# Another plan of products, and the second mixing three steps after the first

## The chip, the cores and the metric

The kernel runs on one core of one Trainium2 chip. The metric is the device time of one execution in microseconds. TensorE (PE in the profile) multiplies, VectorE (DVE), ScalarE (ACT) and GpSimd (POOL) work on elements, SyncE (SP) issues most of the transfers. A matmul writes to PSUM, a memory of eight banks; "PEld" in the rows is the loading of a stationary operand.

## What is computed

Talking-heads attention over 4 batches, 12 heads, 448 positions and a head size of 64, and behind it a feed-forward block with a squared ReLU:

```python
scores = scale * np.matmul(q, k.transpose(0, 1, 3, 2))
scores = np.einsum('bhij,hg->bgij', scores, w_pre)      # first mixing, over heads
scores = scores - np.max(scores, axis=-1, keepdims=True)
attn = np.exp(scores)
attn = attn / (np.sum(attn, axis=-1, keepdims=True) + 1e-09)
attn = np.einsum('bhij,hg->bgij', attn, w_post)         # second mixing, over heads
x = np.matmul(attn, v)          # then to (4 * 448, 768)
h = x @ w_in                    # (768, 2048)
r = np.maximum(h, 0.0)
out = (s * (r * r) + b) @ w_out
```

All inputs and the output are float32. To keep that accuracy the kernel splits operands into a high and a low part and forms each product as three matmuls (low x high, high x low, high x high).

## The kernel before

The 448 query rows of a batch are cut into 4 chunks of 110 or 118 rows, 16 chunks in all, and a chunk into 11 or 12 **blocks** of up to 10 rows. There are 180 blocks; 10 rows times 12 heads give the 120 partitions on which both mixings work. `first[c]` is the first block of chunk c; the last chunk, 15, begins at block 168.

The work on a block t, in order:

- `relayout` (a transfer) and `split` (two GpSimd operations) bring its scores to 120 partitions, as `hl`.
- `premix(t)`, the first mixing: three matmuls into a PSUM slot `pm`; VectorE takes the maximum (L570, "reduction" in the text), ScalarE the exponential (L575) with its sum, and a small scaling of that sum, `st` (L579).
- `normalize(t)`: VectorE's reciprocal (L587), then ScalarE writes the high half of `eh` (L589). `remainder(t)`: VectorE writes the low half of `eh` (L596), the last reader of the `pm` slot. There are three `pm` slots, two from block 168 on.
- `postmix(t)`, the second mixing: twelve small matmuls from `eh` into a slot `po` (L611). `evacuate(t)` copies `po` into the chunk's tile `A`, on VectorE (L627), for the last chunk on ScalarE (L625).

The products that feed and follow the blocks belong to pairs of heads: `qk_pair` (QK in the text) makes scores of a coming chunk in the two PSUM banks `sc`, from which ScalarE copies them to `S` (L495); `av_pair` (AV) multiplies a finished chunk with the values, into `xp`; `prep_q` and `prep_k` transpose Q and K on TensorE, also through `sc`: ScalarE copies the high part out (L444, L464) and VectorE subtracts for the low part (L233), which stays in the list `later` until the next call of `low_parts`. Q of a chunk is transposed in two halves, of four and of two pairs of heads. `head_piece` is a part of the first feed-forward product. `convert_step` issues one operation of the conversion of weights, on VectorE: one per step from step 12 on for seven units of weights, and three per step from step 169 on for three further units.

One loop runs over steps s. Its body, for a step in the middle, issues in this order, and each engine runs what it is given in that order:

```python
        relayout(s + LD); split(s + LS)        # 5 and 2 blocks ahead
        convert_step(NU_EARLY); normalize(s - 1)
        low_parts()
        evacuate(s - 3)
        premix(s)
        remainder(s - 1)
        run_plan(s, True)                      # transfers
        postmix(s - 2)
        run_plan(s, False)                     # transpositions, QK, AV, head pieces
```

What `run_plan` issues in a step stands in a list `plan`, which is made ahead by a small planner: each product has a step at which it is due, the earliest and the last step, and a cost; a step takes products, in order of their due times, while `spent` is below `FILL`. A step may be left without any product ("empty" in the text).

## Time and profile before

| | |
|---|---|
| time, three runs | median 989.76 us (988.83 to 989.76) |
| the profiled execution | 989.5 us, its span 987.8 us |
| TensorE busy | 935.6 us, mean granted clock 0.987 of full |
| VectorE, ScalarE, GpSimd busy | 641.9, 607.9, 399.3 us |
| first reduction of a block | at 32.03 us |
| first AV of the last chunk | at 510.89 us |

The time of an execution is a little longer than its span, which goes from the first to the last instruction. The block steps lie between about 30 and 511 us of the span; behind them follow the feed-forward products. Busy time of TensorE counts matmuls, which overlap, with modelled ends, so what a step costs there is better read from the starts of its matmuls.

### The profile page before, as it was taken

The numbers are of one execution on the slowest core, as the hardware profiler recorded it, in microseconds if no ns is written. First come the engines' busy times: TensorE is split into PE (matmuls) and PEld (weight loads), VectorE is DVE, ScalarE is ACT, GpSimd is POOL, SyncE is SP. The second block draws the span as 40 slices with busy tenths as digits, with TensorE's granted clock in tenths as the row PEclk, the third lists the DMA queues.
The fourth block names the chain that finished last, engine by engine and source line by source line (L and its number), as shares of the span: only waits on it lengthen the run. The fifth ranks groups of instructions, "written<-read, shape, count | busy, mean of one in ns | idle before, by whom it ended". The sixth has DMA issues, their size and how long they took to land.

```text
span 987.8 us, 19819 instructions
## 1 busy us (share of the span) xinstructions
PE 935.6 (95%) x7500; PEld 792.3 (80%) x7500; DVE 641.9 (65%) x1314; ACT 607.9 (62%) x1315; POOL 399.3 (40%) x469
## 2 busy tenths in 40 slices
PE   6798999989999999999799999999999999999998
PEld 3566777757777677777578999899998999999998
DVE  4689999977877787888945605937624911748411
ACT  3587878877888788887658778622215687721000
POOL 2666667756676666767423333200001232310000
PEclk9899999999999999999799999999999999999999
DMA  3565544664346543544511412325441330236521
GB/s 87 150 177 140 142 126 132 173 153 128 103 123 159 131 134 102 141 128 136 168 56 38 142 34 77 92 91 158 134 155 33 106 119 1 64 113 187 164 94 53
DMA packets 124222, 114.63 MB, mean 116 GB/s; under 512 B 61626, under 2 KB 120014, under 8 KB 124126
## 3 DMA queue, kind: packets, MB, share of 16 engines
q1 hardware_dynamic: 115902, 102.26, 37.3%
q10 hardware_dynamic: 8064, 11.01, 3.1%
q8 instruction: 59, 0.97, 0.4%
q0 software_dynamic: 160, 0.09, 0.2%
q14 instruction: 37, 0.30, 0.1%
HBM read 58.28 MB, written 16.52 MB: 76 GB/s over the span
## 4 chain that ended last, share of the span: by engine, by line
PE 52%; ACT 21%; DVE 18%; DMA 5%; issue 2%; SPq 1%; POOL 1%; ACTq 0%; DVEq 0%; POOLq 0%
PE po L300 23%; PE ph L248 16%; ACT pm L575 6%; ACT S L495 5%; DVE st L570 4%; PE xp L509 4%; PE pm L568 3%; DVE A L627 3%; ACT eh L589 3%; ACT st L579 2%; DMA blk<-S 2%; PE sc L485 2%; PE po L611 2%; DVE eh L596 2%; DVE raw L172 1%
## 5 line engine op out<-in xcount | busy, mean ns | idle before, releaser
L300 PE MATMUL po<-w,g 128*128 128x384 f32 x1344 | 234.6, 336 | 2.6 <-ACT h L256 2.6
L300 PEld LDWEIGHTS po<-w,g 128*128 128x128 f32 x1344 | 233.6, 188 | 3.3 <-ACT h L256 3.2
L556 POOL TENSOR_TENSOR hl<-blk,hl 120x448 fp32r<-120x448 f32 x180 | 207.5, 1153 | 15.0
L266 POOL TENSOR_TENSOR g<-h,g 128x448 fp32r<-128x448 f32 x64 | 77.2, 1206 | 293.9 <-ACT g L265 275.4
L555 POOL TENSOR_SCALAR hl<-blk 120x448 fp32r<-120x448 f32 x180 | 105.0, 583 | 158.3 <-PE pm L568 137.4
L248 PE MATMUL ph<-x,w 128*128 128x448 f32 x810 | 166.2, 364 | 0.0
L611 PEld LDWEIGHTS <-eh 120*128 120x128 f16 (+1 forms) x2160 | 118.0, 99 | 56.0 <-DVE eh L596 27.0
L248 PEld LDWEIGHTS ph<-x,w 128*128 128x128 f32 x810 | 152.0, 188 | 12.2
L611 PE MATMUL po<-wpost,eh 120*128 120x120 f16 (+1 forms) x2160 | 148.2, 220 | 10.5 <-DVE eh L596 10.2
L575 ACT ACTIVATE pm<-pm,st 120x448 f32<-120x448 f32 x180 | 109.7, 609 | 76.3 <-DVE st L570 75.4
L596 DVE SCALAR_TENSOR_TENSOR eh<-pm,st,eh 120x448 f16<-120x448 f32 x180 | 122.1, 678 | 15.0 <-ACT eh L589 10.9
L589 ACT ACTIVATE eh<-pm,st 120x448 f16<-120x448 f32 x180 | 114.5, 636 | 15.2 <-DVE st L587 14.2
L570 DVE TENSOR_REDUCE st<-pm 120x1 f32<-120x448 f32 x180 | 110.8, 616 | 11.5 <-PE pm L568 10.9
L627 DVE COPY A<-po 128x480 f32<-128x480 f32 x168 | 107.3, 639 | 0.1
L568 PE MATMUL pm<-hl,wpre_hi 120*120 120x448 f32 x360 | 104.4, 372 | 1.8 <-POOL hl L556 1.8
L485 PE MATMUL sc<-Tk,Tq 64*110 64x448 f32 (+1 forms) x576 | 84.9, 401 | 13.1 <-ACT S L495 6.1
L509 PE MATMUL xp<-A,v 128*64 128x110 f32 (+1 forms) x1536 | 92.3, 266 | 1.0 <-ACT xs L523 1.0
L154 ACT ACTIVATE mk<-raw 128x384 f32<-128x384 f32 x64 | 35.4, 553 | 92.8 <-DMA raw<-in_moe_w_out_dram 38.1
L568 PE MATMUL pm<-hl,wpre_lo 120*120 120x448 f32 x180 | 84.3, 468 | 5.9 <-DVE eh L596 5.3
L495 ACT ACTIVATE S<-sc 110x896 f32<-110x896 f32 (+1 forms) x90 | 82.1, 912 | 8.8 <-PE sc L485 5.4
L509 PEld LDWEIGHTS xp<-A,v 128*64 128x64 f32 x1536 | 74.8, 137 | 15.7 <-issue 8.5
L568 PEld LDWEIGHTS pm<-hl,wpre_hi 120*120 120x120 f32 x360 | 67.0, 187 | 7.2 <-POOL hl L556 2.8
(72 smaller groups left out, 971.3 us busy)
## 6 DMA issues: line engine op xcount, KB each, us to landing
blk<-S SPq DMA_DIRECT2D x172, 210.0 KB
raw<-in_moe_w_in_dram SPq DMA_DIRECT2D x32, 384.0 KB
raw<-in_moe_w_out_dram SPq DMA_DIRECT2D x32, 384.0 KB
xraw<-xd SPq DMA_DIRECT2D x48, 224.0 KB
part<-ob ACTq DMA_DIRECT2D x28, 192.0 KB
acc<-part SPq DMA_DIRECT2D x28, 192.0 KB
out_dram<-acc ACTq DMA_DIRECT2D x28, 192.0 KB
v<-in_v_dram SPq DMA_DIRECT2D x24, 192.0 KB
```

The source lines that it names most:

```text
L248: nc.tensor.matmul(ph[:, :S], w[:, i, c0:c0 + P], x[:, y, :], start=(kc == 0 and m == 0), stop=(kc == NKC - 1 and m == 2),)
L300: nc.tensor.matmul(po[:, :NO], g[:, x, c0:c0 + P], w[:, y, :], start=(f == 0 and m == 0), stop=(f == NF - 1 and m == 2),)
L495: nc.scalar.activation(s_t[ci][:n, 2 * p:2 * p + 2, :], x_t["two"][:n, :, :S], AF.Copy, scale=SCALE)
L509: nc.tensor.matmul(xp[e * D:(e + 1) * D, p % 4, :n], vt[:, e, c, :], a[:, c, 2 * p + e, :n], start=(c == 0), stop=(c == NC - 1),)
L556: nc.gpsimd.tensor_tensor(out=hl[:n, 1, :], in0=blk[:n], in1=hl[:n, 0, :].bitcast(F32), op=ALU.subtract)
L568: nc.tensor.matmul(pm[:n, :S], w[:n, :n], hl[:n, x, :], start=(m == 0), stop=(m == 2))
L570: nc.vector.tensor_reduce(out=st[:n, 0:1], in_=pm[:n, :S], axis=AX.X, op=ALU.max, negate=True)
L575: nc.scalar.activation(e[:n], e[:n], AF.Exp, bias=st[:n, 0:1], accum_out=pm[:n, S:S + 1])
L589: nc.scalar.activation(eh[:n, 0, :], e[:n], AF.Copy, scale=st[:n, 3:4])
L596: nc.vector.scalar_tensor_tensor(out=eh[:n, 1, :], in0=e[:n], scalar=st[:n, 3:4], in1=eh[:n, 0, :], op0=ALU.mult, op1=ALU.subtract,)
L611: nc.tensor.matmul(po[:, c * BP:(c + 1) * BP], eh[:n, x, j0:j0 + P], wpost[:n, y].rearrange("p g i -> p (g i)"), start=(m == 0), stop=(m = ...
L627: nc.vector.tensor_copy(dst, src)
```

## The change

The second mixing of a block, `postmix`, is issued three steps after the first mixing instead of two, and `evacuate` four instead of three; the loop has one step more, and the bounds of the AV pairs and head pieces are one step later. `eh` has three buffers instead of two, and the transposed K tiles `Tk` seven instead of eight. The planner has other costs, and a product is taken if half its cost still fits under `FILL`, where before it was taken while anything was left. No operation is added or removed.

```diff
--- before.py
+++ after.py
@@ -440,7 +440,7 @@
                 nat[:n, c].rearrange("p h d -> p (h d)"),
                 ident[:n, :n],
             )
-        t = qkp.tile([P, 2, S], F32R, tag="Tk", name=f"Tk_{b}_{p}", bufs=8)
+        t = qkp.tile([P, 2, S], F32R, tag="Tk", name=f"Tk_{b}_{p}", bufs=7)
         nc.scalar.activation(t[:, 0, :], tr[:, :S], AF.Copy)
         later.append((t[:, 1, :], tr[:, :S], t[:, 0, :]))
         k_t[b, p] = t
@@ -585,7 +585,7 @@
         n = blocks[t][2] * H
         e, st = e_t[t]
         nc.vector.reciprocal(st[:n, 3:4], st[:n, 2:3])
-        eh = blkp.tile([BP, 2, S], F16, tag="eh", name=f"eh_{t}", bufs=2)
+        eh = blkp.tile([BP, 2, S], F16, tag="eh", name=f"eh_{t}", bufs=3)
         nc.scalar.activation(eh[:n, 0, :], e[:n], AF.Copy, scale=st[:n, 3:4])
         eh_t[t] = eh
 
@@ -628,8 +628,9 @@
 
     LD, LS = 5, 2
     CONV0 = 12
-    FILL = 1.33
-    QK_COST, AV_COST = 0.8, 1.3
+
+    FILL = 1.2
+    QK_COST, AV_COST, PREP_COST = 0.9, 0.95, 0.5
     LATE = 6
 
 
@@ -649,7 +650,7 @@
         step = math.floor(step)
         while load.keys() & {step - 1, step, step + 1}:
             step -= 1
-        load[step] = 0.375
+        load[step] = PREP_COST
         at(step, 1, f, *args)
         return step
 
@@ -672,10 +673,10 @@
             fill.append((when, lo, w1 - 1, QK_COST, 1, qk_pair, (ci, p)))
     for ci in range(NCH):
         b = chunks[ci][0]
-        w0 = first[ci + 1] + 3
-        w1 = first[ci + 2] + 3 if ci + 2 <= NCH else NB + 100
+        w0 = first[ci + 1] + 4
+        w1 = first[ci + 2] + 4 if ci + 2 <= NCH else NB + 100
         if ci == NCH - 1:
-            w0 = NB + 3
+            w0 = NB + 4
         for p in range(NP):
             when = w0 + p * min(w1 - w0, 12) / NP
             fill.append((when, w0, w1 - 1, AV_COST, 1, av_pair, (ci, p)))
@@ -684,13 +685,14 @@
     w0 = first[NCH - 1] + 3
     for i in range(NHEAD * NKC):
         if i < NHEAD * NKC - LATE:
-            when = w0 + i * (NB + 3 - w0) / (NHEAD * NKC - LATE)
-            fill.append((when, w0, NB + 2, 0.567, 1, head_piece, ()))
+            when = w0 + i * (NB + 4 - w0) / (NHEAD * NKC - LATE)
+            lo = first[NCH - 1] + max(4, 2 + min(i, NKC - 1))
+            fill.append((when, lo, NB + 3, 0.567, 1, head_piece, ()))
         else:
-            fill.append((NB + 100, NB + 3, NB + 100, 0.567, 1, head_piece, ()))
+            fill.append((NB + 100, NB + 4, NB + 100, 0.567, 1, head_piece, ()))
     fill.sort(key=lambda x: x[0])
     spent, closed = 0.0, {}
-    for s in range(NB + 4):
+    for s in range(NB + 5):
         spent = max(spent, -0.4) + load.get(s, 0)
         left, held = [], set()
         for x in fill:
@@ -698,12 +700,12 @@
             waits = f in held
 
             opens = f is qk_pair or (f is av_pair and args[1] % 4 == 0)
-            if opens and closed.get(f, -1) >= s and s <= NB + 2 and s < hi:
+            if opens and closed.get(f, -1) >= s and s <= NB + 3 and s < hi:
                 waits = True
 
             if f is qk_pair and s in load and s < hi:
                 waits = True
-            if not waits and lo <= s and (s > NB + 2 or hi <= s or (x[0] < s + 4 and spent < FILL)):
+            if not waits and lo <= s and (s > NB + 3 or hi <= s or (x[0] < s + 4 and spent + cost / 2 <= FILL)):
                 at(s, order, f, *args)
                 spent += cost
                 if f is qk_pair or (f is av_pair and args[1] in (3, NP - 1)):
@@ -772,7 +774,7 @@
         x[3](*x[4])
         low_parts()
     tail = first[NCH - 1]
-    for s in range(NB + 3):
+    for s in range(NB + 4):
         if s == tail - LD:
             early.close()
             rp = ctx.enter_context(tc.tile_pool(name="rp", bufs=1, side="right", reuse_waits="tile"))
@@ -791,15 +793,15 @@
                     convert_step(NU_EARLY + 3)
             normalize(s - 1)
         low_parts()
-        if 0 <= s - 3 < NB:
-            evacuate(s - 3)
+        if 0 <= s - 4 < NB:
+            evacuate(s - 4)
         if s < NB:
             premix(s)
         if 0 <= s - 1 < NB:
             remainder(s - 1)
         run_plan(s, True)
-        if 0 <= s - 2 < NB:
-            postmix(s - 2)
+        if 0 <= s - 3 < NB:
+            postmix(s - 3)
         run_plan(s, False)
         if 0 <= s - (tail - LD) < NKC:
             load_x(0, 0, s - (tail - LD))
```

TensorE's order at a change of batch, steps 62 and 63 (the steps begin at the rows `pm`, the first mixing; `po` is the second mixing, of which one row stands here; `trk` a transposition of K, `sc` a QK pair, `xp` an AV pair). Before:

```order
L568 MATMUL pm_3112<-hl_3010,wpre_lo 120x448
L568 MATMUL pm_3112<-hl_3010,wpre_hi 120x448 x2
...
L438 MATMUL trk_3_3138<-ident,nk_3_2852 128x128 x3
L438 MATMUL trk_3_3138<-ident,nk_3_2852 128x64
L568 MATMUL pm_3155<-hl_3063,wpre_lo 120x448
L568 MATMUL pm_3155<-hl_3063,wpre_hi 120x448 x2
...
L485 MATMUL sc_0_3178<-Tk_0_1355,Tq_3046 118x448 x6
L509 MATMUL xp_4_3186<-A_2435,v_4_2917 64x110 x8
```

The same two steps of the change:

```order
L568 MATMUL pm_3080<-hl_2974,wpre_lo 120x448
L568 MATMUL pm_3080<-hl_2974,wpre_hi 120x448 x2
...
L438 MATMUL trk_3_3106<-ident,nk_3_2815 128x128 x3
L438 MATMUL trk_3_3106<-ident,nk_3_2815 128x64
L509 MATMUL xp_0_3017<-A_2445,v_2_2751 64x110 x8
L568 MATMUL pm_3131<-hl_3033,wpre_lo 120x448
L568 MATMUL pm_3131<-hl_3033,wpre_hi 120x448 x2
...
L485 MATMUL sc_0_3154<-Tk_0_1331,Tq_3010 118x448 x6
```

The AV pair now stands behind the transposition, ahead of the next first mixing, and the QK pair of step 63 is alone.

TensorE's order where a chunk's AV pairs begin, steps 103 to 105. Before:

```order
L568 MATMUL pm_4912<-hl_4819,wpre_lo 120x448
...
L568 MATMUL pm_4944<-hl_4862,wpre_lo 120x448
...
L509 MATMUL xp_0_4966<-A_4433,v_0_4542 64x110 x8
L509 MATMUL xp_0_4966<-A_4433,v_1_4629 64x110 x8
L568 MATMUL pm_4997<-hl_4905,wpre_lo 120x448
...
L460 MATMUL trq_0_5024<-ident,nq_4739 128x118 x4
L509 MATMUL xp_0_4966<-A_4433,v_2_4716 64x110 x8
```

The same steps of the change:

```order
L568 MATMUL pm_4886<-hl_4782,wpre_lo 120x448
...
L485 MATMUL sc_5_4908<-Tk_5_3952,Tq_4495 110x448 x6
L568 MATMUL pm_4929<-hl_4840,wpre_lo 120x448
...
L568 MATMUL pm_4961<-hl_4879,wpre_lo 120x448
...
L460 MATMUL trq_0_4988<-ident,nq_4712 128x118 x4
L509 MATMUL xp_0_4994<-A_4442,v_0_4552 64x110 x8
```

Before, step 103 is empty and step 104 holds two AV pairs; in the change a QK pair stands in step 103, step 104 is empty and step 105 holds one AV pair.

VectorE's order in step 170, in the last chunk (from its reduction on; L176, L178 and L155 are conversion, `x_0_2` the low part of an input of the feed-forward block). Before:

```order
L570 TENSOR_REDUCE st_7785<-pm_7781 120x1
L596 SCALAR_TENSOR_TENSOR eh_7777<-pm_7742,st_7746,eh_7777 120x448
L176 TENSOR_SCALAR u_7733<-w_7731 128x384
L178 SCALAR_TENSOR_TENSOR w_7731<-raw_2685,u_7733 128x384
L155 TENSOR_SCALAR u_7819<-raw_3014 128x384
L587 RECIPROCAL st_7785<-st_7785 120x1
L233 TENSOR_TENSOR x_0_2_7804<-xraw_0_2_7611,x_0_2_7804 128x448
L570 TENSOR_REDUCE st_7831<-pm_7827 120x1
```

The same of the change:

```order
L570 TENSOR_REDUCE st_7771<-pm_7767 120x1
L596 SCALAR_TENSOR_TENSOR eh_7763<-pm_7728,st_7732,eh_7763 120x448
L176 TENSOR_SCALAR u_7719<-w_7717 128x384
L178 SCALAR_TENSOR_TENSOR w_7717<-raw_2660,u_7719 128x384
L155 TENSOR_SCALAR u_7804<-raw_2978 128x384
L587 RECIPROCAL st_7771<-st_7771 120x1
L233 TENSOR_TENSOR x_0_2_7789<-xraw_0_2_7597,x_0_2_7789 128x448
L627 COPY A_7374<-po_7776 128x48x10
L570 TENSOR_REDUCE st_7816<-pm_7812 120x1
```

One evacuation more runs on VectorE here, since the evacuation of the last chunk, which is ScalarE's, begins a step later.

## Rows read from the trace of the kernel before

**Rows 1.** The page's first part: busy us of each engine, share of the span, instructions.

```profile
PE 935.6 (95%) x7500; PEld 792.3 (80%) x7500; DVE 641.9 (65%) x1314; ACT 607.9 (62%) x1315; POOL 399.3 (40%) x469
```

**Rows 2.** Busy time by stretches: length; PE, PEld, DVE, ACT, POOL; clock; transfers' share, GB/s.

```profile
63.91:157.58 93.67, 87.92 (x965) 64.34 (x964) 86.93 (x186) 75.70 (x182) 61.73 (x70) 1.00 0.50 135
...
250.37:315.15 64.78, 63.58 (x730) 47.80 (x728) 51.98 (x110) 52.55 (x128) 44.46 (x58) 1.00 0.48 125
```

**Rows 3.** Groups between 63.91 and 466.95: busy, mean ns | idle before, releaser.

```profile
L611 PE MATMUL po<-wpost,eh 120*128 120x120 f16 x1788 | 119.8, 217 | 6.9 <-DVE eh L596 6.7
...
L570 DVE TENSOR_REDUCE st<-pm 120x1 f32<-120x448 f32 x148 | 91.1, 616 | 6.3 <-PE pm L568 5.8
...
L587 DVE RECIPROCAL st<-st 120x1 f32<-120x1 f32 x149 | 24.1, 162 | 37.8 <-ACT st L579 37.6
...
L485 PE MATMUL sc<-Tk,Tq 64*118 64x448 f32 x144 | 21.0, 395 | 6.0 <-DVE Tk L233 4.3 <-ACT S L495 1.4 <-DVE Tq L233 0.3
```

**Rows 4.** Timeline, two steps: start, length, engine, line, [idle before, releaser].

```profile
211.42 0.61 DVE L570 TENSOR_REDUCE st<-pm 120x1 f32<-120x448 f32 x1
...
212.07 0.61 ACT L575 ACTIVATE pm<-pm,st 120x448 f32<-120x448 f32 x1 [1.26 <-DVE st L570]
...
213.07 0.16 DVE L587 RECIPROCAL st<-st 120x1 f32<-120x1 f32 x1 [0.44 <-ACT st L579]
213.15 0.64 DVE L627 COPY A<-po 128x480 f32<-128x480 f32 x1
213.70 0.61 DVE L570 TENSOR_REDUCE st<-pm 120x1 f32<-120x448 f32 x1
...
216.89 0.61 DVE L570 TENSOR_REDUCE st<-pm 120x1 f32<-120x448 f32 x1
```

**Rows 5.** Timeline, the reductions around a second half of a Q transposition.

```profile
264.51 0.62 DVE L570 TENSOR_REDUCE st<-pm 120x1 f32<-120x448 f32 x1
...
267.27 0.61 DVE L570 TENSOR_REDUCE st<-pm 108x1 f32<-108x448 f32 x1
```

**Rows 6.** Timeline, first and last of the 156 reductions of blocks 13 to 168.

```profile
65.75 0.61 DVE L570 TENSOR_REDUCE st<-pm 120x1 f32<-120x448 f32 x1
...
469.58 0.61 DVE L570 TENSOR_REDUCE st<-pm 120x1 f32<-120x448 f32 x1
```

**Rows 7.** Timeline, a reduction that waited for its first mixing.

```profile
221.99 0.62 DVE L570 TENSOR_REDUCE st<-pm 120x1 f32<-120x448 f32 x1 [0.45 <-PE pm L568]
```

**Rows 8.** Timeline of TensorE, steps 102 (a QK), 103 (empty), 104 (two AV).

```profile
300.95 0.47 PE L568 MATMUL pm<-hl,wpre_lo 120*120 120x448 f32 x1
...
303.17 0.47 PE L568 MATMUL pm<-hl,wpre_lo 120*120 120x448 f32 x1
...
303.88 0.80 PE L611 MATMUL po<-wpost,eh 120*128 120x120 f16 x12
304.50 0.44 PE L568 MATMUL pm<-hl,wpre_lo 120*120 120x448 f32 x1
...
305.67 0.80 PE L611 MATMUL po<-wpost,eh 120*128 120x120 f16 x12 [0.33 <-DVE eh L596]
...
308.07 0.47 PE L568 MATMUL pm<-hl,wpre_lo 120*120 120x448 f32 x1
```

**Rows 9.** Last chunk: busy time of a stretch (as rows 2); timeline, two first mixings.

```profile
475.00:480.00 5.00, 4.18 (x22) 2.99 (x23) 4.93 (x13) 3.43 (x9) 1.77 (x3) 0.50 0.40 141
...
474.90 0.70 PE L568 MATMUL pm<-hl,wpre_lo 120*120 120x448 f32 x1 [2.88 <-DVE eh L596]
...
478.39 0.70 PE L568 MATMUL pm<-hl,wpre_lo 120*120 120x448 f32 x1 [0.82 <-DVE eh L596]
```

**Rows 10.** Timeline: last first mixing, last second mixing, AV of the last chunk.

```profile
504.67 0.37 PE L568 MATMUL pm<-hl,wpre_lo 108*108 108x448 f32 x1
...
509.45 0.80 PE L611 MATMUL po<-wpost,eh 108*128 108x120 f16 x12 [0.39 <-DVE eh L596]
...
510.89 3.45 PE L509 MATMUL xp<-A,v 128*64 128x118 f32 x64
```

## The prediction

> **What bounds the kernel now.** I read the page's busy shares first: TensorE 95% of the span, VectorE 65%, ScalarE 62% [rows 1]. That looks like a TensorE bound, but it mixes two stages. The change touches only the block steps, so I cut that stage out by the rows of its reductions (one per block) and read the engines in it. In the first 94 us TensorE is busy 87.92 and VectorE 86.93 of 93.67; in a later stretch, 250 to 315 us, it is 63.58 against 51.98 of 64.78 [rows 2]. So TensorE has little idle time, and VectorE has little too as long as weight conversions run on it.
>
> Then I read what the engines wait for in this stage. TensorE's second mixing waits 6.9 us for VectorE's remainder `eh`, and that is the wait the lag of three is aimed at. VectorE's reduction waits only 6.3 us, 5.8 of them for the first mixing. VectorE's reciprocal, however, waits 37.8 us for ScalarE's `st` [rows 3]. A wait that recurs so evenly (149 reciprocals) belongs to a loop, and the timeline shows it [rows 4]: the reduction at 211.42 releases the exponential (212.07), then the sum `st`, the reciprocal (213.07, after 0.44 us of waiting); behind the reciprocal in VectorE's order stand the evacuation copy (213.15) and only then the next block's reduction (213.70). That is a period of **2.28 us** which no step undercuts by more than 0.04. If a transposition was made in the step, its low part stands in front of the evacuation and waits for ScalarE's copy: 213.70 to 216.89, 3.19 us, so 0.91 more. The second half of a Q transposition is smaller: 264.51 to 267.27 is 2.76, 0.48 more [rows 5].
>
> From block 13 to block 168 the reductions start at 65.75 and 469.58: 403.8 us for 155 steps [rows 6]. The loop alone asks for 155 x 2.28 + 31 x 0.91 (18 K transpositions, 13 first halves of Q) + 13 x 0.48 = 353.4 + 28.2 + 6.2 = 387.8. So **16.0 us is all that this stretch can lose** while the loop stays as it is. I went through its 155 periods: in 30 steps the reduction began within 0.95 us of its own first mixing, which means that VectorE had been waiting for TensorE; such a place is 221.99, idle 0.45 [rows 7]. These 30 steps carry 8.2 us over the loop price. The other 7.8 us lie in steps where TensorE was in time: 1.5 in one step whose score copy waits for a DMA, about 2.5 around transpositions that came late because the `sc` bank was still being emptied, the rest in steps with conversions.
>
> TensorE's own price: a step without a product takes 303.17 to 304.50, 1.33 us; with a QK pair 300.95 to 303.17, 2.22; with two AV pairs 304.50 to 308.07, 3.57, of which 0.33 is a wait for `eh` and the issue after it [rows 8]. So QK costs 0.89 and AV about 0.92 to 1.0. A step with one QK and one AV is 3.1 us against a loop period of 2.28: TensorE must enter it 0.9 us ahead, or the loop starves.
>
> **The change, part by part.**
>
> *Lag of three.* It removes no instruction. Before, the second mixing of step s needs the remainder of block s-2, which VectorE writes just after the reduction of s-1. So TensorE can run at most about 1.7 us ahead of the loop before it stands at `eh`. With three steps that stop goes; the next one is the first mixing's PSUM slot (three slots, free after the remainder of s-2), some 0.65 us further on, which is the second mixing's 0.62 us (303.88 to 304.50, [rows 8]). The 6.9 us of waits are therefore not 6.9 us of gain. Where the loop was late anyway they cost nothing (before the empty steps 163 to 168 TensorE waits at `eh` while the period is 2.28). What counts is the starved steps. The third `eh` buffer makes the write of `eh` wait for the same distance as before, so it costs nothing; the `Tk` ring of seven still has a slot for each transposition whose last reader stands earlier on TensorE, at least one step ahead.
>
> *The even plan.* It moves QK, AV and the transpositions between steps without adding one. Pairs of AV in one step (3.57) become single ones; after a K transposition an AV now stands where nothing stood, and the QK that used to share the next step with that AV is alone. Before, QK waited for the low part of `Tk`, 4.3 us in the chunks of 118 rows [rows 3]; now 0.92 us of AV covers that. If it did not, the old waits would return. The loop prices do not change.
>
> *Sum over the 155 steps.* Of the 8.2 us in starved steps about 4.0 lie where TensorE has idle time in reserve (the stretches with K transpositions, and the first 50 steps); I take 90% of it, 3.6. The other 4.2 lie in stretches like the second of [rows 2], where TensorE is idle for only 1.2 of 64.78 us and cannot get far ahead; I take half, 2.1. Of the 2.5 us of late transpositions I take 1.5. Together **7.2 us**. Bounds: 3 (only the starved steps of the stretches with reserve, mostly) and 12 (three quarters of 16.0).
>
> *The last chunk.* Here the price runs the other way. From step 169 VectorE has three conversion operations per step and is busy 4.93 of 5 us; the first mixing waits 2.88 us for it, and TensorE's clock falls to 0.50 of full, its 1.2 GHz level [rows 9]. The evacuation moves to ScalarE at block 168; one step more of lag leaves one more copy on the full VectorE: 213.15 to 213.70, **0.55 us**. The AV pairs of chunk 14 start at step 172 rather than 171, so step 171 is empty, and work that stood in VectorE-bound steps now stands behind the last first mixing. Before, from 504.67 to the first AV of the last chunk at 510.89 it is 6.2 us [rows 10]. After, one second mixing (0.62) and one AV (0.92) more stand there, and the wait before 510.89 for the last evacuation has no head piece under it. I take **1.5 us**, since the added work also fills the 0.39 us wait at 509.45. Bounds of the whole: 0 (the work is only moved) and 3.9 (one full VectorE-bound step, 474.90 to 478.39, and half a microsecond).
>
> *The start.* Steps 0 to 12 keep their plan, and the first score copies there wait for transfers: 0.
>
> Sum: -7.2 + 0.55 + 1.5 = **-5.2 us** on the profiled execution's 989.5 (span 987.8 and 1.7 around it), 0.26 below the median of 989.76. So 984.3.
>
> **Rivals.** *The starved steps only change their cause (little or no change).* In the second stretch of [rows 2] TensorE is busy for 98%; if a stall freed at `eh` comes back at the `sc` bank or the PSUM slot, only 2 to 3 us are left, and the last chunk takes 2: 988.7. For it: QK also waits for the previous copy out of `sc` (1.4 us in the chunks of 118 rows [rows 3]), and the plan still has a QK right before most transpositions. Against: the waits that precede starved steps are mostly those at `eh` and `Tk`.
>
> *VectorE is full in the first stretch.* It is busy 93% there, so a TensorE that is early finds nothing to win: 2.0 us of starved steps and 0.5 of late transpositions fall out of the sum: 986.8. The Trainium skill ("Perfetto Trace Analysis", section "Identifying the Most-Contended Engine") would judge VectorE by its occupancy and TensorE by its weight-load share rather than by its busy share; by that VectorE (93% against 64.34 of 93.67, 69%) is the engine to relieve, and this change relieves it of nothing. In the later stretch the same reading finds no full engine at all, which is what a latency loop looks like.
>
> *Slower.* The place is the clock in the last chunk. It fell while TensorE stood for lack of work and came back only after TensorE had been busy without a pause. With step 171 empty too, the low level may hold over the first filled steps: each microsecond of their work that runs at 1.2 instead of 2.4 GHz costs one more. If steps 172 and 173 (about 5 us of work) run low in addition, the last chunk costs 7 instead of 2 us, and with the lower bound of 3 before it the time is 993.5. With the main gain at its lower bound it decides from about 3 us of additional low-clock work on.
>
> *More than forecast.* The `sc` waits go too and the last chunk costs nothing: 12 us, 977.5.
>
> **How the numbers follow.** Chances: the forecast 0.50 (by itself 981 to 987), VectorE full 0.20, little or none 0.14, more 0.08, slower 0.08. Range 977.5 to 990.5: it leaves out half of "more" and most of "slower". A measurement of this kernel can tell about 0.2%, 2 us, from no change. Faster by more than that (below 987.8): the forecast, most of "VectorE full" and "more", 0.75; within: 0.16; slower: 0.09.
>
> **What would show it.** The period of the loop stays 2.28 and 3.19. The idle time of the reduction for the first mixing falls from 5.8 to below 3 us; the waits of the second mixing for `eh` before step 168 are gone. Block 13 to block 168 takes 396 to 397 us instead of 403.8; from the reduction of block 168 to the first AV of the last chunk it is 43.4 instead of 41.3. I am wrong if the period itself moves, if the starved steps stay about 30, or if the low clock of the last chunk lasts more than a step longer.

## The result: slower by 0.57%, and the profile after

The change takes 994.61 us (median of 6 runs, 992.91 to 997.39) against 989.84 for the kernel before, timed beside it. The ratio is 1.0057, 95% interval 1.0044 to 1.007. The forecast of 984.3 was wrong in sign, and the time lies outside its range. The profiled execution took 993.91 us with a span of 992.2.

The page's first part hardly differs from [rows 1] (TensorE is busy for 936.8 us instead of 935.6); the same work is done in a longer span.

The two stretches of [rows 2], from the same first mixing to the same first mixing (blocks 13 to 48 and 82 to 108), in the same columns. They took 93.67 and 64.78 us before:

```profile
62.52:157.16 94.64, 87.14 (x960) 64.24 (x958) 88.16 (x188) 75.44 (x182) 62.11 (x71) 1.00 0.50 136
249.63:315.22 65.59, 64.49 (x736) 48.22 (x735) 52.16 (x110) 53.85 (x130) 44.50 (x58) 1.00 0.48 127
```

Groups between the first mixings of blocks 13 and 168, as in [rows 3]. The score copy (L495), the transposition of Q (L460) and the QK of the chunks of 110 rows are groups to which the prediction gave no line:

```profile
L611 PE MATMUL po<-wpost,eh 120*128 120x120 f16 x1788 | 120.0, 217 | 1.4 <-DVE A L627 1.4
...
L570 DVE TENSOR_REDUCE st<-pm 120x1 f32<-120x448 f32 x148 | 91.0, 615 | 7.5 <-PE pm L568 7.4
...
L485 PE MATMUL sc<-Tk,Tq 64*110 64x448 f32 x326 | 46.9, 391 | 4.8 <-DVE Tk L233 2.1 <-DVE Tq L233 1.9 <-ACT S L495 0.8
...
L495 ACT ACTIVATE S<-sc 118x896 f32<-118x896 f32 x24 | 21.9, 911 | 5.6 <-DMA blk<-S 3.3 <-DMA nk<-in_k_dram 2.3
L485 PE MATMUL sc<-Tk,Tq 64*118 64x448 f32 x144 | 20.9, 395 | 4.6 <-DVE Tk L233 3.1 <-ACT S L495 1.2
...
L460 PE MATMUL trq<-ident,nq 118*128 118x118 f32 x24 | 4.1, 283 | 6.9 <-ACT S L495 6.9
```

These three in the kernel before:

```profile
L485 PE MATMUL sc<-Tk,Tq 64*110 64x448 f32 x326 | 46.9, 392 | 2.6 <-ACT S L495 1.9
...
L495 ACT ACTIVATE S<-sc 118x896 f32<-118x896 f32 x24 | 21.9, 911 | 1.7 <-DMA xd<-xs 1.7
...
L460 PE MATMUL trq<-ident,nq 118*128 118x118 f32 x24 | 4.0, 275 | 1.2 <-ACT S L495 1.2
```

The waits of the second mixing at `eh` are gone, 6.7 us to none, as forecast. But the reduction does not wait less for the first mixing: 7.4 us instead of 5.8. The QK of the chunks of 110 rows waits longer, 4.8 us instead of 2.6, mostly for VectorE's low parts. New are two waits: ScalarE's score copy `S` stands 5.6 us for transfers (1.7 before), and behind it TensorE's transposition of Q stands 6.9 us (1.2 before). The two places, in the timeline:

```profile
202.15 0.92 ACT L495 ACTIVATE S<-sc 118x896 f32<-118x896 f32 x1 [2.50 <-DMA blk<-S]
203.12 0.42 PE L460 MATMUL trq<-ident,nq 118*128 118x118 f32 x2 [3.19 <-ACT S L495]
...
203.47 1.73 PE L509 MATMUL xp<-A,v 128*64 128x110 f32 x16
...
321.75 0.57 POOL L555 TENSOR_SCALAR hl<-blk 120x448 fp32r<-120x448 f32 x1 [3.10 <-DMA blk<-S]
321.83 0.92 ACT L495 ACTIVATE S<-sc 118x896 f32<-118x896 f32 x1 [2.27 <-DMA nk<-in_k_dram]
...
322.80 0.57 PE L460 MATMUL trq<-ident,nq 118*128 118x118 f32 x2 [2.97 <-ACT S L495]
```

These are steps 64 and 109, each two steps behind the first transposition of K for the next batch (62 and 107). They last 6.72 and 6.65 us from first mixing to first mixing. Behind each stand of TensorE its granted clock is at the lower level (1.2 GHz), as two stretches in the columns of [rows 2] show:

```profile
203.46:206.87 3.41, 3.41 (x25) 2.65 (x25) 2.04 (x5) 2.36 (x7) 0.64 (x2) 0.50 0.52 137
322.93:326.34 3.41, 3.41 (x22) 2.37 (x23) 1.81 (x4) 2.57 (x7) 0.60 (x1) 0.50 0.48 127
```

So a stall costs more than its wait. The AV pair at 203.47 takes 1.73 us; without the stall the same pair takes 0.97 (shown below, with late stores).

The reductions of blocks 13 and 168 answer to [rows 6]:

```profile
64.36 0.61 DVE L570 TENSOR_REDUCE st<-pm 120x1 f32<-120x448 f32 x1
...
472.73 0.61 DVE L570 TENSOR_REDUCE st<-pm 120x1 f32<-120x448 f32 x1
```

That is 408.4 us where 403.8 stood and 396 to 397 was forecast: +4.5, as much as the whole loss in the span (+4.4). I worked through the 155 periods as for the prediction, each less its loop price. "Starved" means that the reduction began within 0.95 us of its own first mixing.

| blocks 13 to 168, us over the loop price of 387.8 | starved steps | other steps | sum |
|---|---|---|---|
| before | 32, 8.2 | 7.8 | 16.0 |
| change | 21, 6.5 | 14.0 | 20.5 |

(I count 32 steps now instead of 30; the two more lie at the limit of 0.95 and carry nothing, the sum is the same.) The starved steps gain 1.7, and the others lose 6.2, nearly all of it in the steps that wait for `S`: 64, 109 and 153 lie 3.6, 3.5 and 0.8 us over the loop price in the change, and 1.5, 0.3 and 0.0 before. So there are two questions: where does the new wait come from, and why do the freed waits at `eh` give so little?

### The profile page after: what moved, and what is told of

It reads as the page before. It is cut to its first block, busy times and chain, and to the rows that moved or that the text cites. A ratio compares the mean times of both kernels' runs of the same rounds, so it can differ in the third digit from the quotient of the medians.

```text
span 992.2 us, 19958 instructions
## 1 busy us (share of the span) xinstructions
PE 936.8 (94%) x7500; PEld 794.4 (80%) x7500; DVE 638.9 (64%) x1314; ACT 608.9 (61%) x1315; POOL 398.4 (40%) x469
## 4 chain that ended last, share of the span: by engine, by line
PE 62%; ACT 14%; DVE 11%; DMA 7%; POOL 2%; SPq 2%; issue 2%; ACTq 0%; DVEq 0%; POOLq 0%
PE po L300 23%; PE ph L248 16%; PE pm L568 7%; PE po L611 5%; PE xp L509 5%; DMA blk<-S 4%; PE sc L485 4%; ACT pm L575 4%; ACT S L495 3%; DVE st L570 2%; DVE A L627 2%; ACT st L579 1%; ACT eh L589 1%; POOL hl L556 1%; DMA raw<-in_moe_w_out_dram 1%
## 5 line engine op out<-in xcount | busy, mean ns | idle before, releaser
L509 PE MATMUL xp<-A,v 128*64 128x110 f32 (+1 forms) x1536 | 96.0, 269 | 1.6 <-ACT xs L523 1.0
L495 ACT ACTIVATE S<-sc 110x896 f32<-110x896 f32 (+1 forms) x90 | 82.1, 912 | 13.7 <-PE sc L485 5.1
```

The lines of the kernel that those rows point to most:

```text
L509: nc.tensor.matmul(xp[e * D:(e + 1) * D, p % 4, :n], vt[:, e, c, :], a[:, c, 2 * p + e, :n], start=(c == 0), stop=(c == NC - 1),)
```

## The experiments

Each was timed beside the kernel before on the same chip, which had medians of 988.2 to 989.8; ratios are to it. For a look at the block steps I use the time from the reduction of block 13 to that of block 168, since the first reduction alone comes anywhere between 30.1 and 33.6 us in these runs.

### Which half of the change, and are the value loads to blame?

The score copy must wait because the tile `S` has two buffers: the first QK of chunk c overwrites the scores of chunk c-2, and the `relayout` transfers that read them must have landed. SyncE issues these transfers in a fixed order with the loads of K, Q and V and with the stores `xd` of finished AV pairs. The change puts AV work one step later, and the value loads with it. In the expectations A says that those loads, one step later, stand ahead of the last relayout; B that it is the lag; C that it is the new order of products.

**v_back** puts the value loads back to their old steps:

```diff
-                at(w0 + (p + 1) * (w1 - w0) / NP, 2, load_v, b + 1, p)
+                at(w0 - 1 + (p + 1) * (w1 - w0) / NP, 2, load_v, b + 1, p)
```

> The change, with the loads of the next batch's values issued one step earlier, at the steps they had before. Theory A (those loads now stand in SyncE's queue ahead of the last relayout of a chunk; that transfer lands about 2 us later, the score copy into the other S buffer waits for it and ScalarE stands): the stall of step 109 (4.1 us over the step's price) falls below 0.5, that of step 64 (4.2) to 1.5 to 3, and the time to 988 to 990.5. Theory B (the loss is the lag itself: second mixing, evacuation and AV one step later): the time stays at 993 to 996. Theory C (the loss is the new order of products, QK right before transpositions in the one sc slot): stays too, 993 to 996.

Measured: 996.39 us, ratio 1.0072 (1.0059 to 1.0085). TensorE's waits for `S` at steps 64 and 109 stayed (3.85 and 2.20 us; 3.19 and 2.97 in the change). One step of the value loads is not the cause.

**v_none** leaves out the value loads of batches 1 to 3; AV then uses the values of batch 0:

```diff
-        a, vt = a_t[ci], v_t[b, p]
+        a, vt = a_t[ci], v_t[0, p]
...
-                at(w0 + (p + 1) * (w1 - w0) / NP, 2, load_v, b + 1, p)
+                pass
```

> The change without the loads of values for batches 1 to 3 (all batches use those of batch 0, so the output is another one). Theory A: the stalls of steps 64 and 109 are both below 1 us and the time is 985 to 988. Theories B and C: the products, the order on the engines and the lag are the same, so 992 to 996.

Measured: 985.12 us, ratio 0.9966 (0.9954 to 0.9978), blocks 13 to 168 in 400.5 us. Without the values of 18 pairs the stalls fall from 4.2 and 4.1 us over TensorE's price of the step to 0.9 and 1.0. So it is the transfers, but it could be their bytes or their places in SyncE's order.

**plan_only** has the new costs and rule with the lag of two:

```diff
-    w0 = first[ci + 1] + 4
+    w0 = first[ci + 1] + 3
...
-            evacuate(s - 4)
+            evacuate(s - 3)
...
-            postmix(s - 3)
+            postmix(s - 2)
```

> The new planner costs and rule with the lag of two (two eh buffers, eight Tk, all bounds at their old steps, so the value loads too). Theory A: no long stall at 109; the waits of the second mixing for eh come back in part, 987 to 990.5. Theory B: no loss either, 985 to 990. Theory C: 993 to 996.

**lag_only** has the old costs and rule with the lag of three:

```diff
-    FILL = 1.2
-    QK_COST, AV_COST, PREP_COST = 0.9, 0.95, 0.5
+    FILL = 1.33
+    QK_COST, AV_COST = 0.8, 1.3
...
-            if not waits and lo <= s and (s > NB + 3 or hi <= s or (x[0] < s + 4 and spent + cost / 2 <= FILL)):
+            if not waits and lo <= s and (s > NB + 3 or hi <= s or (x[0] < s + 4 and spent < FILL)):
```

> The old planner costs and rule with the lag of three (and with it AV pairs and value loads one step later). Theory A: the long stalls of the score copies at 64 and 109 stand here too, 992 to 996. Theory B: 993 to 996 without such stalls, the loss spread over the steps. Theory C: the loss is gone, 987 to 990.5.

Measured: plan_only 990.95 us, ratio 1.0025 (1.0016 to 1.0034), blocks 13 to 168 in 406.1; lag_only 994.75, ratio 1.0053 (1.004 to 1.0066), 410.8. The stalls at steps 64 and 109 stand in lag_only too (2.8 and 2.7 us over the loop price), as theory A said of it. The lag makes most of the loss; the plan alone makes a small one and lies in none of the three ranges. Neither gains.

### SyncE's queue

SyncE's own waits say more. This is the costliest of them from 60 to 470 us, in the change: waiting instruction, its releaser, us in total, times, longest.

```profile
SPq L528 <- ACT xs L523: 81.7, 24, 5.1
```

It is the `xd` store, which waits for the scaled AV result `xs`. In the kernel before it is already there:

```profile
SPq L528 <- ACT xs L523: 77.8, 21, 5.8
```

The store is issued in the program right behind its AV pair, but SyncE comes to it up to 5.1 us, some two steps, before the result is there, and holds everything behind it. Here is SyncE ahead of step 109 in the change:

```profile
288.98 0.80 SPq L548 DMA_DIRECT2D blk<-S  x1
294.58 0.38 SPq L528 DMA_DIRECT2D xd<-xs  x1
...
312.65 2.63 SPq L390 DMA_DIRECT2D nk<-in_k_dram  x2
...
317.39 1.76 SPq L548 DMA_DIRECT2D blk<-S  x2
```

From 289.78 to 294.58 it issues nothing; from 294.58 on it issues without a pause, since loads of K, Q and V for coming steps are due now. It does not catch up in time. The first transfer at 317.39 is the last relayout of the chunk whose scores the copy overwrites. The score copy starts at 321.83, 4.4 us behind its issue. (The row above names a K load as what ended its wait; GpSimd's split of that relayout's block, which starts at 321.75 when `blk` has come, shows that the relayout landed at the same time.) Before, the store that stood longest in this stretch came earlier:

```profile
281.41 0.81 SPq L548 DMA_DIRECT2D blk<-S  x1
287.25 0.38 SPq L528 DMA_DIRECT2D xd<-xs  x1
...
315.23 0.82 SPq L548 DMA_DIRECT2D blk<-S  x1
...
319.55 0.92 ACT L495 ACTIVATE S<-sc 118x896 f32<-118x896 f32 x1 [0.26 <-DMA xd<-xs]
```

There the hold ended at 287.25, before most of the loads, and the same relayout was issued at 315.23; the score copy started at 319.55 after 0.26 us of waiting. With the lag of three and the new plan, the AV pairs of the first 13 chunks and their stores come one to three steps later in the program while the relayouts keep their steps. Theory D: the change loses its time because a waiting store holds a queue that has no slack where the loads for a next batch fall due. Theory E: the bytes of the value loads fill the transfer engines. Late stores tell them apart, since they leave every byte as it is. The edit, used in four kernels, issues each `xd` store two steps later in SyncE's order (at once in the last two chunks); `store_due` stands in the loop behind the last `run_plan` and issues what has stood in the list `stores` for two steps:

```diff
-            nc.sync.dma_start(
-                xd[b][p0:p + 1, :, n0:n0 + n].rearrange("a p n -> p a n"), xs[:, p0:p + 1, :n]
-            )
+            stores.append((x_t["step"], xd[b][p0:p + 1, :, n0:n0 + n].rearrange("a p n -> p a n"), xs[:, p0:p + 1, :n]))
+            if ci >= NCH - 2:
+                store_due(x_t["step"])
...
+        store_due(s - 2)
```

**store_late** is the change with it:

> The change, with each xd store (SyncE, after the fourth and the sixth AV pair of a chunk) issued two steps later in SyncE's order. Theory D (SyncE reaches such a store about two steps before its AV pair is done and holds everything behind it, waits of 4 to 5 us; at a change of batch its queue is full of loads and doesn't catch up before the chunk's last relayout, whose late landing stops the score copy and with it ScalarE): the stalls at steps 64, 109 and 153 are below 1.2 us each, SyncE's wait of xd for xs falls from 104.6 to below 60 us, and the time is 985 to 988.5. Theory E (not the issue but the bytes of the value loads in the transfer engines make that relayout land late): the bytes are the same, so the stalls stay and the time is 992 to 996.

**b_store_late** is the kernel before with it:

> The kernel before, with the xd stores issued two steps later. Theory D: it has such a stall only at step 64 (1.3 us), so 986 to 989. Theory E: no change, 988 to 990.

**lag_store_late** and **plan_store_late** are lag_only and plan_only with it:

> The old plan with the lag of three, with the xd stores issued two steps later. Theory D: what the lag cost is gone, 986 to 990. Theory E: 992 to 996 as without the edit.

> The new plan with the lag of two, with the xd stores issued two steps later. Theory D: about 1 us less than without the edit, 987.5 to 990.5; the plan's own loss of 1 to 2 us stays. Theory E: 990 to 992 as without the edit.

| kernel | ratio as it is | with late stores, us (ratio) | blocks 13 to 168, us, as it is and with late stores |
|---|---|---|---|
| before | 1 | 985.41 (0.997, 0.9959 to 0.998) | 403.8, 401.9 |
| change | 1.0057 | 985.27 (0.9975, 0.9967 to 0.9984) | 408.4, 401.0 |
| plan_only | 1.0025 | 986.87 (0.9987, 0.9977 to 0.9996) | 406.1, 403.6 |
| lag_only | 1.0053 | 986.94 (0.9987, 0.9978 to 0.9996) | 410.8, 402.8 |

D holds and E falls: with the same bytes the ratio of the change falls by 0.8% (8 us), that of lag_only by 0.7%, plan_only by 0.4% and the kernel before by 0.3%. In the change with late stores the wait for `xs` between 60 and 470 us falls from 81.7 to 0.7 us, the score copy hardly waits (0.6 us), and steps 64 and 109 last 3.72 and 3.54 us instead of 6.72 and 6.65, with the granted clock at its full level. SyncE's wait, the AV pair of step 64, and the groups (the store now stands in L537, and line numbers from L548 on are 7 higher):

```profile
SPq L537 <- ACT xs L523: 0.7, 2, 0.5
```

```profile
202.45 0.97 PE L509 MATMUL xp<-A,v 128*64 128x110 f32 x16
```

```profile
L618 PE MATMUL po<-wpost,eh 120*128 120x120 f16 x1860 | 124.5, 217 | 1.7 <-DVE A L634 1.7
...
L577 DVE TENSOR_REDUCE st<-pm 120x1 f32<-120x448 f32 (+1 forms) x154 | 94.8, 615 | 5.4 <-PE pm L575 5.4
...
L495 ACT ACTIVATE S<-sc 110x896 f32<-110x896 f32 (+1 forms) x79 | 72.0, 912 | 0.6 <-DMA blk<-S 0.2
```

The kernel before and plan_only gained more than theory D had said (986 to 989 and 987.5 to 990.5). But the change with late stores is not faster than the kernel before with late stores (their intervals overlap nearly whole), and either half by itself is 0.2% behind it (the intervals just overlap). The reduction waits 5.4 us for its first mixing where that kernel has 5.9. So the gain that I forecast was not only hidden by the queue; most of it is not there.

### Why the freed waits give little

With late stores the periods can be compared without the queue. The table is worked out as the one above, by stretches; each entry is starved steps, other steps, in us over the loop price, all with late stores:

| steps | before | change | lag of three, old plan | new plan, lag of two |
|---|---|---|---|---|
| 13 to 48 (conversions run) | 1.5, 3.5 | 0.8, 4.2 | 1.0, 5.4 | 1.3, 3.5 |
| 48 to 63 (conversions run) | 0.6, 1.0 | 0.4, 1.9 | 0.3, 1.3 | 0.8, 1.1 |
| 63 to 82, 108 to 127, 150 to 168 | 2.5, 1.1 | 1.4, 0.6 | 1.7, 2.7 | 1.9, 1.6 |
| 82 to 108, 127 to 150 (mostly AV, QK and Q transpositions) | 3.7, 0.2 | 3.7, 0.2 | 2.6, 0.1 | 5.4, 0.1 |
| sum | 8.3, 5.8 | 6.3, 6.9 | 5.6, 9.4 | 9.4, 6.3 |

The last stretches do not move in the change, but each half of it moves them. The lag alone gains 1.1 us there (0.5 of it in steps 82 to 108, with the same 13 QK and 15 AV pairs as before), so the waits at `eh` did cost something. The new plan alone loses 1.7: it puts 14 QK pairs instead of 13 into each of the two, the one more taken out of the stretch ahead; at 0.89 us each by [rows 8] that is 1.8. Together they cancel. The QK matmuls (six to a pair) in steps 82 to 108, the lag alone and behind it the change, both with late stores:

```profile
L485 PE MATMUL sc<-Tk,Tq 64*110 64x448 f32 x78 | 11.2, 392 | 0.9 <-ACT S L495 0.9
...
L485 PE MATMUL sc<-Tk,Tq 64*110 64x448 f32 x84 | 12.1, 391 | 1.1 <-DVE Tq L233 0.6 <-DVE Tk L233 0.5
```

What is left there is mostly TensorE's own work. The change with late stores at step 101, a QK and an AV in one step; TensorE and the reductions:

```profile
296.01 0.47 PE L575 MATMUL pm<-hl,wpre_lo 120*120 120x448 f32 x1
...
297.06 0.61 DVE L577 TENSOR_REDUCE st<-pm 120x1 f32<-120x448 f32 x1
297.45 0.87 PE L485 MATMUL sc<-Tk,Tq 64*110 64x448 f32 x6
298.26 1.03 PE L509 MATMUL xp<-A,v 128*64 128x118 f32 x16
299.22 0.47 PE L575 MATMUL pm<-hl,wpre_lo 120*120 120x448 f32 x1
...
300.12 0.62 DVE L577 TENSOR_REDUCE st<-pm 120x1 f32<-120x448 f32 x1 [0.69 <-PE pm L575]
```

TensorE waits for nothing here. It enters the step 1.05 us before the reduction, which is 0.15 more than the shortest distance there is (0.90, at the end of the step), and the step takes 3.21 us. It has little time to get ahead: over the 23 to 26 steps of such a stretch the first mixing is ahead of its reduction by 1.2 to 1.3 us on average in the kernel before and in the change; with the lag alone it is 1.3 to 1.4.

In the first stretch other waits took the place of those at `eh`. Two steps of the change as it is, 17 and 37 (`po` waits for an evacuation, `sc` for the low part of `Tk`, both VectorE's work):

```profile
73.33 0.81 PE L611 MATMUL po<-wpost,eh 120*128 120x120 f16 x12 [0.76 <-DVE A L627]
...
130.09 0.85 PE L485 MATMUL sc<-Tk,Tq 64*110 64x448 f32 x6 [1.13 <-DVE Tk L233]
```

VectorE is busy 88.16 of 94.64 us there. Theory F says that this is why the stretch gains nothing; theory G that it is the order of the products, a QK right behind a transposition. The test issues the early conversions in every second step, so that they last to about step 110 and not to about step 61:

```diff
-            if s >= CONV0:
+            if s >= CONV0 and s % 2 == 0:
                 convert_step(NU_EARLY)
```

**sl_half_conv** is the change with late stores and this, **bsl_half_conv** the kernel before with both.

> The change with late stores, and the early weight conversions issued in every second step (to about step 110) instead of in every step (to about step 61). Nothing is left out. Theory F (the first stretch gains nothing because VectorE is full there): with half the conversions per step the waits of TensorE for VectorE's low parts and evacuations between step 15 and 48 go, and from the first mixing of block 13 to that of block 48 it takes 2 to 4 us less than the 94.7 us with all conversions, and less than the kernel before with the same edit. Theory G (it is the order of the products: a QK pair right behind a transposition, whatever VectorE does): the waits for Tk at steps 18 and 37 stay near 1.1 us and the stretch stays near 94.7. After step 61 VectorE has one operation of about 0.5 us more in every second step; by F that costs up to 1 us up to step 110. Whole time by F 983 to 984 us, by G 985 to 986.

> The kernel before with late stores and the same half rate of conversions. Theory F: it gains as well, but less in the first stretch (93.5 us with all conversions; 92 to 93 expected), since its waits at eh stay, so the change is ahead of it by 1 us or more from block 13 to 168 than it was at the full rate (0.9 us). Theory G: it stays at 93.5, and the difference between the two stays 0.9 us from block 13 to 168. Whole time 984 to 985.5 us.

Measured from first mixing 13 to first mixing 48, with late stores: the kernel before 93.52 us at the full rate and 92.33 at half; the change 94.69 and 92.69. From block 13 to 168 the change led by 0.9 us at the full rate (401.0 against 401.9) and by 2.3 at half (400.1 against 402.4). In the same stretch of sl_half_conv VectorE is busy 87% and not 93%:

```profile
64.92:157.61 92.69, 86.98 (x959) 64.19 (x958) 80.29 (x171) 73.58 (x179) 61.58 (x71) 1.00 0.47 127
```

The wait at step 37 went, the one at step 18 stayed at 1.21 us, and waits of 1.21 us stand at steps 63 and 108 too, where a QK is the first work behind a transposition that has its step to itself. So F holds in kind: half the conversions give the change 2.0 us in this stretch and the kernel before 1.2. (The same edit in the last experiment below gives 1.5, so the difference between the two kernels is not sure.) F's mark that the change be ahead of the kernel before there missed, it is 0.4 behind; the waits of 1.21 us are those of G, and the half rate leaves them. From block 13 to 168 the half rate gives the change 0.9 us and costs the kernel before 0.5: conversions now stand in steps 82 to 108, where the steps that are not starved cost 1.9 us instead of 0.1 in both. The time as a whole did not follow: 986.31 (ratio 0.9979, 0.997 to 0.9987) and 986.42 (0.9971, 0.9961 to 0.9982), neither below the full rate. In the profiled run of the first the first reduction came at 33.56 us.

**sl_evac** tests the term of the last chunk: in the change with late stores, block 167 is evacuated on ScalarE.

```diff
-        if ci == NCH - 1:
+        if t >= first[NCH - 1] - 1:
             nc.scalar.activation(dst, src, AF.Copy)
```

> The change with late stores, and the evacuation of block 167 on ScalarE rather than VectorE, so that VectorE's first step with three conversions has no evacuation more than before. If the term of 0.55 us for that copy in the last chunk is right, the first AV of the last chunk comes 0.5 us earlier relative to the first mixing of block 168; if other engines bound these steps, nothing changes. Whole time 0 to 0.6 us below the change with late stores (985.3).

Measured: 984.83 us, ratio 0.996 (0.9948 to 0.9972). From the first mixing of block 168 to the first AV of the last chunk it takes 43.5 us, 45.0 without the edit and 43.9 in the kernel before with late stores. Step 171, which VectorE bounds, shortened from 3.54 to 2.97 us, by the copy of 0.55. The rest lies in step 172, 5.50 us without the edit and 4.62 with it, and there the granted clock differs. Step 172 without the edit and with it, in the columns of [rows 2]:

```profile
478.29:483.79 5.50, 5.50 (x35) 4.16 (x35) 5.23 (x12) 3.75 (x10) 1.80 (x2) 0.50 0.61 194
...
477.39:482.01 4.62, 4.62 (x35) 3.54 (x35) 4.55 (x10) 3.23 (x8) 2.32 (x3) 0.62 0.70 219
```

In v_none and v_back, which have this step as the change has it, it takes 4.60 and 4.89 us. So the term of 0.55 is right, and that the other 0.9 us come from the copy is not shown.

**sl_evac_half** puts late stores, half the rate and this evacuation together:

> The change with late stores, half the rate of early conversions and the evacuation of block 167 on ScalarE; nothing is left out. If the three add up and the late first reduction of the half-rate run (33.56 us, other runs 30.1 to 32.0) was chance: first reduction near 31, reductions of blocks 13 to 168 in 400.1 us (full rate 401.1), from there as in the run with the evacuation alone, 983 to 984.5 us. If the half rate itself delays the start, the first reduction comes at 33 again and the time is 986.

Measured: 984.45 us, ratio 0.9961 (0.9947 to 0.9974); first reduction at 31.11, blocks 13 to 168 in 400.5 us. The stretch from first mixing 13 to 48 takes 93.12 us, against 94.64 in sl_evac. The late start of the half-rate run did not come again, so the half rate does not bring it by itself, and the half rate gives nothing that can be measured in the whole time. The version to keep is one with late stores; the kernel before and the change have the same 0.3% from them, and the evacuation on ScalarE may add 0.1%, which the intervals do not tell from nothing.

## Why the prediction was wrong, step by step

**The step that failed: "Lag of three. It removes no instruction."** I followed only TensorE, VectorE and ScalarE. The lag moves the AV pairs, and each pair takes its `xd` store and value loads along in SyncE's order, past the relayouts, which stay. This queue has no row in the prediction; the one step "whose score copy waits for a DMA" (1.5 us) was its first sign, and I put it down as a loss of before rather than as a place without slack. Measured in the change: 6.2 us in the other steps between blocks 13 and 168, at steps 64, 109 and 153, part of it by the lower clock behind the stalls. As the late stores show, the queue costs the change 8 us of the whole time, of which the kernel before already lost 3.

**The main gain, 7.2 us, was mis-sized by itself.** With the queue out of the way its three terms are these. Starved steps where TensorE has idle time: 3.6 forecast, 2.0 measured. Starved steps in the full stretches: 2.1 forecast ("I take half"), 0.0 measured: the lag gains 1.1 there, and the plan takes it back. *The even plan* was priced at nothing because it "moves QK, AV and the transpositions between steps without adding one"; it moves a QK pair into each stretch where TensorE is full. Late transpositions and conversions: 1.5 forecast as a gain, 1.1 measured as a loss. The sum is 0.9, below my lower bound of 3. That bound held the stretches with reserve to be safe, and the first 50 steps were not: VectorE is full in them.

**The rivals.** "VectorE is full in the first stretch" was right as a mechanism: the stretch took 94.64 us instead of 93.67, and half the conversions gave back 1.5 to 2.0 us of it to the change and 1.2 to the kernel before. By its occupancy, as the Trainium skill reads it ("Perfetto Trace Analysis", section "Identifying the Most-Contended Engine"), VectorE was the engine to relieve, and in this stretch these runs agree; the whole time did not follow. "The starved steps only change their cause" was right for the rest: `A`, `Tk` and `Tq` took the place of `eh`. The slower rival was not it in the place it named: the last chunk costs 1.0 us in all (below), and behind its first AV the two kernels differ by 0.4 us (477.4 and 476.9 to the end of the span). Its mechanism, work at the lower clock behind a stand of TensorE, came at steps 64 and 109 instead. The rival that came true, a store that holds SyncE's queue, was not among them.

**What was right.** The loop kept its periods, 2.28 and 3.18 us, as three reductions of the change show:

```profile
222.31 0.61 DVE L570 TENSOR_REDUCE st<-pm 120x1 f32<-120x448 f32 x1
...
225.49 0.61 DVE L570 TENSOR_REDUCE st<-pm 120x1 f32<-120x448 f32 x1
...
227.77 0.61 DVE L570 TENSOR_REDUCE st<-pm 120x1 f32<-120x448 f32 x1
```

The waits of the second mixing at `eh` before block 168 went. The even plan's AV did not cover the low part of `Tk` in the chunks of 118 rows, though: 4.3 us became 3.1, and 2.1 stand in those of 110 rows.

**The last chunk, +2.05 forecast.** From the first mixing of block 168 to the first AV of the last chunk the change takes 44.92 us instead of 43.94, so +1.0. v_none, v_back and the change with late stores, which have the change's order there, take 44.0, 44.3 and 45.0, so this is sure to about 1 us only. The rows of the first mixings at which steps 170 to 172 begin answer to [rows 9]; each waits for VectorE's remainder:

```profile
477.76 0.70 PE L568 MATMUL pm<-hl,wpre_lo 120*120 120x448 f32 x1 [4.10 <-DVE eh L596]
...
481.25 0.70 PE L568 MATMUL pm<-hl,wpre_lo 120*120 120x448 f32 x1 [0.82 <-DVE eh L596]
...
484.79 0.70 PE L568 MATMUL pm<-hl,wpre_lo 120*120 120x448 f32 x1 [0.87 <-DVE eh L596]
```

The granted clock is at the lower level there for 13.65 us, exactly as long as in the kernel before. The whole of that stretch, before and in the change, in the columns of [rows 9]:

```profile
471.12:484.77 13.65, 9.95 (x63) 7.74 (x59) 12.38 (x26) 8.99 (x22) 4.36 (x5) 0.50 0.55 175
...
476.53:490.18 13.65, 10.74 (x64) 8.12 (x64) 13.42 (x30) 8.83 (x22) 5.22 (x6) 0.50 0.61 192
```

Before, it began behind waits of 0.76 and 0.83 us, ahead of the 2.88 us of [rows 9], and covered step 171, the first with an AV pair and a head piece (5.55 us). In the change it covers step 172, now the first (5.48 us). So the low clock moved with the work and did not last longer. From the last first mixing (506.87) to the first AV of the last chunk (514.84) it is 8.0 us, 1.75 more than [rows 10] give, where 1.5 was forecast; but the steps ahead of it hold one AV pair less (four between the first mixings of blocks 168 and 179, five before), which the term of 1.5 does not subtract. So the whole is half of what was forecast, within its bounds.

What stays open: the starved steps that could be freed where TensorE has reserve (1.4 us are left), why the lag with the old plan costs 1.9 and 1.6 us more in the steps that are not starved (13 to 48, and the stretches with K transpositions), and what the lag is worth with a plan that keeps QK pairs out of the full stretches; no run tried a third plan.

## What to carry to other kernels

When a change moves work, list what travels with it in every in-order queue, SyncE's too, and look there for an instruction that waits: a store issued beside its producer holds all loads behind it, and a later producer makes that hold later. A store that nobody reads soon is best issued some steps behind its producer. And the sum of an engine's waits is not what their removal gives: 6.7 us of waits went, and with the queue out of the way 0.9 us were gained. Count the gain by stretches, and check in each what work the change moves into it: one pair of products more took the gain back where TensorE was full, and where VectorE was full other waits took its place.

## What the runs showed of the hardware

SyncE can be without slack while the transfer engines have some: from 294.58 to 317.39 us it issued without a pause, one relayout of 210 KB in about 0.8 to 0.9 us and a pair of K loads in up to 2.6, while the packets of its queue took only about half of the transfer engines' time. The queues from 288 to 324 us show it (packets, MB, share of 16 engines), in the change and behind it in the kernel before, which moved more in that time:

```profile
q1 hardware_dynamic: 8552, 4.88, 54.9%
...
q1 hardware_dynamic: 9394, 5.64, 61.6%
```

No share of busy time points to this queue; the order of its issues and the gap ahead of them do.

A stand of TensorE can cost more than its length: behind the stands of 3.19 and 2.97 us at steps 64 and 109 the granted clock was 0.50 for 3.41 us each, and with late stores, where TensorE stands 0.95 and 0.77 us there, it stayed full.
